# Half-contraction groups beside the first attention, and q of the second batch transposed on TensorE

## The chip, the cores and the metric

The kernel runs on one NeuronCore of one Trainium2 chip. The core has five engines that run side by side, each with its own instruction queue: TensorE (PE) for matrix products, VectorE (DVE), ScalarE (ACT), GpSimd (POOL) and SyncE (SP). Loads and stores (DMA) are issued by SP, ACT or POOL and are carried out by the core's 16 DMA engines. The metric is the device time of one execution in microseconds (us). Five timed runs of the kernel before gave a median of 305.79 us, from 305.18 to 306.97.

## What is computed

Eight batches of eight heads of linear attention are followed by a two-layer feed-forward network over all 4608 tokens. Cut to what matters:

```python
q_s = softmax(q, axis=-1)            # over the 64 of a head
k_s = softmax(k, axis=2)             # over the 576 positions
kv  = einsum('bhsd,bhse->bhde', k_s, v)
x   = einsum('bhsd,bhde->bhse', q_s, kv)   # then to (4608, 512)
h   = x @ w_in                       # 512 -> 2048
g   = where(h > 0, h, exp(min(h, 0)) - 1)
out = g @ w_out                      # 2048 -> 512
```

Inputs and output are 32-bit floats. The softmaxes are computed without the subtraction of the maximum, and the sum over k is taken as an extra column of ones in v.

## The kernel before

**Units and blocks.** Attention is cut into 16 units: unit n is half of batch n // 2, four heads. The feed-forward part is cut into nine blocks of 512 tokens. A batch has 576 tokens in nine chunks of 64, so the first block needs the first eight chunks of batch 0, and the second block the last chunk of batch 0 and most of batch 1.

**Elementwise work of a unit.** `q_part` takes the exp of q in place (ACT, L351), sums each row (DVE, L358) and takes the reciprocal (L363); `q_mul` multiplies and writes 16-bit QS (DVE, L374). `k_part` takes the exp of k (ACT, L394) and casts v to 16 bits, on POOL (L400) or on DVE (L403). To stand as a right-hand side, q must have its features on the partitions. For units 0 and 1 `tp` does that on PE: nine 128x128 transposes against an identity matrix (L420) into PSUM, and two evictions to qsT (L428). For all later units `q_mul` issues a DMA transpose on SP (L378), and `cvt` converts the result to qsT on POOL (L387).

**kv and attention of a unit.** `kv` does 36 small matmuls (L447); DVE takes the reciprocal of the sums (L460) and writes the scaled products into MBLK (two at L465). `ao` multiplies MBLK with qsT (L488) and evicts the result into XT, by ACT alone (L507) or with one half on ACT (L499) and one on DVE (L503). XT holds x transposed, as four contraction chunks (kc) of 128 features: unit 2b gives kc 0 and 1, unit 2b + 1 gives kc 2 and 3.

**A block.** `hg` makes one of eight groups: for two tiles of 128 hidden features, four matmuls each over kc 0 to 3 (L533), each 128x512. ACT takes exp (L541); POOL takes the minimum with 1 (L546) and DVE the rest of the elu (L549), or, in the first three groups of the first block, DVE does both (L553, L556). Then `out_mm` makes four output tiles, each over 16 hidden tiles (L566), in pieces of four matmuls; `out_store` evicts by ACT (L580) and stores by SP (L586). The next batch's kv and attention are put between the pieces of `out_mm`, at the places that the dictionary `work` gives.

**PSUM.** There are four tensors PS0 to PS3 of two banks each. They go round by name: hg's groups take A, Bs, C, Dd in turn, out takes A and Bs, and kv and attention of the next batch take C and Dd.

**The head.** SP loads q of unit 0 in two halves (L614), then q of unit 1 and k of unit 0 (L302). POOL loads v of unit 0, k and v of unit 1, W1 in twelve pieces (L314), then q2, q3, k2, v2, k3, v3 and W2 in four pieces of 1 MB (L324). PE fills waits with dummy matmuls on the identity (`spin`, L518).

**The order of the work.** Nothing is written out by hand but PE's order: `add` collects operations with a duration, a key and what they depend on, and `order` simulates the five queues with these durations and a model of the DMA rate. Each engine of the other four takes what could start first, and among those within 60 ns the one with the lowest key. Operations called `low` stand back for others that fall due. The resulting order is fixed in each engine's queue; on the chip, an engine that waits holds up all that stands behind it.

Of the kernel before, what the change touches and what calls it, by code (L numbers as in the profile page):

```python
# [19 lines left out]
ISSUE = {"sp": 600, "act": 650, "gp": 760}  # L20
W1CUT = (0, 2, 4, 8)


class Op:
    __slots__ = ("eng", "dur", "emit", "deps", "key", "idx", "start", "end",
                 "dma", "sem", "val", "clock", "nbytes", "follow", "low", "ready", "tag", "port", "slack", "rel")

# [7 lines left out]
class Sched:  # L35
# [5 lines left out]
    PGUARD = 0.3  # L41
    MARGIN = 2500
    DMA_RATE = 388.0
# [4 lines left out]
    def __init__(self, nc):  # L48
        self.nc = nc
        self.E = {"sp": nc.sync, "act": nc.scalar, "dve": nc.vector,  # L50
                  "pe": nc.tensor, "gp": nc.gpsimd}
        self.ops = []
        self.slack = False
        self.rel = None
        self.w = {}
        self.r = {}

    def add(self, eng, dur, emit, key, R=(), W=(), X=(), dma=None, nbytes=0, after=(),
# [3 lines left out]
        op.follow, op.low, op.tag, op.port = follow, low, tag, port  # L62
        op.slack = self.slack and low
        op.rel = self.rel if low else None
# [19 lines left out]
    def hop(self, d, o):  # L84
        if d.dma:
            return 60 + (self.MARGIN if o.slack else 0)
        if d.eng == o.eng:
            return 0 if o.eng == "pe" else 50
        if d.eng == "pe":
            return 210  # L90
        if o.eng == "pe":
            return 120
        return 70
# [32 lines left out]
    def one_pass(self, land):  # L126
# [27 lines left out]
        while left:  # L154
# [33 lines left out]
            if o.dma:  # L188
                o.end = max(s + self.DMA_GO[e] + self.DMA_TAIL + o.nbytes / self.DMA_RATE,
                            land.get(o, 0))  # L190
            out.append(o)
# [59 lines left out]
class Gen:  # L251
# [68 lines left out]
    def load_w2(self, s, key, follow=None):  # L320
        w = self.w_out.rearrange("(jj p) c -> p jj c", p=128)
        sl = slice(s * 4, (s + 1) * 4)
        return self.S.add(
            "gp", ISSUE["gp"], lambda e: e.dma_start(self.W2[:, sl, :], w[:, sl, :]), key,  # L324
            W=[f"W2_{s}"], dma=f"w2{s}", nbytes=1 << 20, follow=follow, tag=f"W2 {s}")

# [40 lines left out]
    def q_mul(self, n, key, dmat):  # L367
# [8 lines left out]
        if dmat:  # L376
            t16 = self.raw_flat(n, "q").bitcast(F16)[:, 0:1152].rearrange("p (c t) -> p c t", c=CH)
            S.add(dmat, 1400, lambda e: e.dma_start_transpose(  # L378
                t16, self.QS[al][:, :, :].rearrange("p c x -> p (c x)")), key,
                R=[f"QS{al}"], W=qR, dma=f"tp{i}{dmat}", nbytes=128 * 2304, low=True, tag=f"dtp{n}")  # L380

# [52 lines left out]
    def kv(self, units, ps, key):  # L434
# [17 lines left out]
        for n in units:  # L452
            i = n % 2
            R += [f"kR{i}", f"VB{i}0", f"VB{i}1", f"VBone{i}"]
        S.add("pe", len(units) * 300 + 330, mm, key, R=R, X=self.banks(ps), tag=f"kv{units}")
        PV = P[:, :].rearrange("p (f x) -> p f x", f=2)
# [21 lines left out]
    def ao(self, n, x, ps, key, evac="act"):  # L478
# [7 lines left out]
        for f in range(2):  # L486
            def mm(e, f=f):
                return e.matmul(P[:, f * 512:f * 512 + n_], M[:, f, :],  # L488
                                T[:, c0:c1, f * 64:f * 64 + 64], start=True, stop=True)
            S.add("pe", 230, mm, key,  # L490
                  R=[f"qsT{n % 2}{y}" for y in range(2)] + [f"MBLK{i}", f"MBLK{i}0", f"MBLK{i}1"],
                  X=[f"b{2 * ps + f}"], tag=f"ao{n}.{x}")
        src = P[:, :].rearrange("p (f t) -> p f t", f=2)[:, :, 0:n_]
        names = lambda f: [f"X{2 * u + f}_{(b * CH + c) % SLOTS}" for c in range(c0, c1)]
        if evac == "split":
            for f, eng in ((0, "act"), (1, "dve")):
# [11 lines left out]
              W=names(0) + names(1), X=self.banks(ps), tag=f"evx{n}")  # L508

    def spin(self, count, bk, after=None):
# [3 lines left out]
        def mm(e):  # L516
            for _ in range(count):
                last = e.matmul(dst, self.ID[:, :], self.ID[:, :], start=True, stop=True)  # L518
            return last
        self.S.add("pe", count * 57, mm, -5, R=["ID"], X=[f"b{bk}"],  # L520
                   after=[after] if after else (), tag="spin")

    def hg(self, j, g, ps, key, pool):
        S = self.S
        P = self.PS[ps]
        rc = BLK * (j % 3)
        xs = [f"X{kc}_{(8 * j + x) % SLOTS}" for kc in range(4) for x in range(8)]

        def mm(e):
            for t in range(2):  # L530
                tt = 2 * g + t
                for kc in range(4):
                    last = e.matmul(P[:, t * 512:(t + 1) * 512],  # L533
                                    self.W1[:, kc, tt * 128:(tt + 1) * 128],
                                    self.XT[:, kc, rc:rc + BLK], start=(kc == 0), stop=(kc == 3))
            return last
        self.pe = S.add("pe", 8 * 227, mm, key, R=xs + [f"W1_{kc}_{g}" for kc in range(4)], X=self.banks(ps), tag=f"hg{j}.{g}")
        i = self.eslot % len(self.ESB)
# [21 lines left out]
    def out_mm(self, jb, ts, bk, jj0, jj1, key):  # L560
# [3 lines left out]
        def mm(e):  # L564
            for jj in range(jj0, jj1):
# [4 lines left out]
              R=[f"G_{g}" for g in range(jj0 // 2, (jj1 + 1) // 2)] +  # L570
                [f"W2_{s}" for s in range(jj0 // 4, (jj1 + 3) // 4)], X=[f"b{bk}"],
              tag=f"out{jb}.{ts}.{jj0}")
# [32 lines left out]
    def program(self):  # L605
# [4 lines left out]
        for h in range(2):  # L610
# [4 lines left out]
                       W=[f"qR0h{h}"], dma=f"q0h{h}", nbytes=128 * 2304, follow=sp, tag="ld q0")  # L615
        for n, t in ((1, "q"), (0, "k")):
            sp = self.load(n, t, "sp", -89, follow=sp)
        gp = self.ident
        for n, t in ((0, "v"), (1, "k"), (1, "v")):
            gp = self.load(n, t, "gp", -80, follow=gp)  # L620
# [9 lines left out]
        self.q_mul(1, -63, None)  # L630
        self.k_part(0, -62)
        self.k_part(1, -64, vconv="dve")
        self.tp(0, 3, -64)
        self.spin(36, 0)
        self.kv([0], 2, -66)
        self.spin(9, 0)
        self.tp(1, 1, -64)
        self.spin(18, 0)
        self.kv([1], 3, -68)
        self.ao(0, 0, 0, -67, evac='split')  # L640
        self.ao(0, 1, 2, -60)
        self.ao(1, 0, 1, -67, evac="split")
        self.spin(6, 0)

        for what in ("2q", "3q", 0, "2k", "2v", 1, 2, "3k", "3v", 3):
            if isinstance(what, int):
                gp = self.load_w2(what, -50, follow=gp)
            else:
                gp = self.load(int(what[0]), what[1], "gp", -50, follow=gp)
        self.ldq, self.w2 = None, [gp]  # L650

        def loads(n, ts, key):
# [3 lines left out]

        def elem_q(b, key):
            for n in (2 * b, 2 * b + 1):
                self.q_part(n, key)
                if b != 2:  # L660
                    self.q_mul(n, key, "sp")

        def elem_k(b, key):
            for n in (2 * b, 2 * b + 1):
                self.k_part(n, key)

# [4 lines left out]
        key = 0  # L671
        A, Bs, C, Dd = 3, 0, 2, 1
        for j in range(NBLK):
            order = [A, Bs, C, Dd]
            for g in range(8):
                self.hg(j, g, order[g % 4], key, j or g > 2)
                key += 1
                if (j, g) == (0, 0):
                    self.ao(1, 1, 2, -66)
                    elem_q(1, 8)  # L680
                    elem_k(1, 8)
                    convert(1, 8)
            if j == 1:
# [8 lines left out]
            if b < B:  # L692
                n0, n1 = 2 * b, 2 * b + 1
                S.slack = True
                if more:
# [5 lines left out]

                def kv(units, b=b, C=C, more=more):
                    self.kv(units, C, key)
                    for n in units:
# [3 lines left out]

                def last(n1=n1, b=b, C=C, more=more):
                    self.ao(n1, 1, C, key)  # L710
                    if more and b > 1:
                        convert(b + 1, k1)
                todo = [lambda n=n0, d=Dd: self.ao(n, 0, d, key), lambda n=n0, c=C: self.ao(n, 1, c, key),
                        lambda n=n1, d=Dd: self.ao(n, 0, d, key), last]
                if j == 0:
                    work = dict(zip((6, 10, 11, 12, 13, 14),
                                    [lambda: kv([2]), lambda: kv([3])] + todo))
                else:
                    work = dict(zip((4, 12, 13, 14, 15) if j == 1 else (3, 6, 8, 9, 11), [lambda u=[n0, n1]: kv(u)] + todo))
            if j == 0:  # L720
                plan = [(ts, jq) for jq in range(4) for ts in range(4)]
            else:
                plan = [(ts + t, jq) for ts in (0, 2) for jq in range(4) for t in range(2)]
            bank = [2 * A, 2 * A + 1, 2 * Bs, 2 * Bs + 1]
            for k, (ts, jq) in enumerate(plan):
                self.out_mm(j, ts, bank[ts], 4 * jq, 4 * jq + 4, key)
                if jq == 3:
                    self.out_store(j, ts, bank[ts], key, last=(j, ts) == (NBLK - 1, 3))
                if k in work:
                    work[k]()  # L730
                key += 0.5
            if j == 0:
# [35 lines left out]
```

## Time and profile before

| what | us |
|---|---|
| median of five timed runs | 305.79 |
| the profiled execution's own time | 307.48 |
| its span, first to last instruction | 305.4 |
| start of the first block's groups (first L533) | 23.67 |
| start of the first out (first L566) | 38.75 |
| start of the second block's groups | 55.72 |
| PE busy over the span | 292.1 |

Times of rows count from the start of the span. In a timeline a row gives the start, the length, the engine, the line, the operation with the tiles that it writes and reads, and a count where several are merged; in brackets stands how long its engine stood idle before it and what ended that. Neighbouring matmuls overlap in such a row, since each is given with its latency. The chain of waits follows back, from the last instruction, what released each piece of work. PEclk is the clock granted to TensorE as a share of full speed.

### The profile page before, as it was taken

Reading aid. Unit: us, or ns where it says so; the run is one execution under the profiler, and the core shown is the slowest. Engines: PE = TensorE matmul, PEld = TensorE weight load, DVE = VectorE, ACT = ScalarE, POOL = GpSimd, SP = SyncE. Lnnn points to the kernel's source line nnn. Section 1 sums busy time; section 2 is a strip of 40 time slices with the busy share of each in tenths; the row PEclk is TensorE's granted clock in tenths of the full one; section 3 lists DMA queues with packets and bytes.
Section 4 is the critical chain, followed back from the end, with each engine's and each line's share of the span. In section 5 each row is a group of like instructions: output and inputs, shape, how many; then the busy total and the mean of one; then the engine's idle time right before and its main releaser. Section 6 shows DMA issues by size and latency. Waiting matters only on the chain.

```text
span 305.4 us, 4546 instructions
## 1 busy us (share of the span) xinstructions
PE 292.1 (96%) x1925; PEld 241.2 (79%) x1925; DVE 149.9 (49%) x181; ACT 151.2 (50%) x179; POOL 125.1 (41%) x128
## 2 busy tenths in 40 slices
PE   6389999999999999999999999999999999999994
PEld 6377878788888888888887888888888888888883
DVE  4345971189816770678057805790463046105600
ACT  3254922784475564565556455635552355125411
POOL 7691552183338422841284228504650045005500
PEclk9869999999999999999999999999999999999998
DMA  7999999950996099108950794069201220130032
GB/s 219 398 400 391 390 249 280 319 223 0 231 321 206 2 345 299 36 0 263 288 129 2 276 300 105 0 201 273 54 0 32 47 61 3 38 80 20 2 69 69
DMA packets 38116, 50.56 MB, mean 166 GB/s; under 512 B 18768, under 2 KB 18768, under 8 KB 38096
## 3 DMA queue, kind: packets, MB, share of 16 engines
q1 hardware_dynamic: 32880, 36.45, 42.8%
q0 software_dynamic: 5136, 13.70, 13.8%
q8 instruction: 15, 0.25, 0.3%
q10 hardware_dynamic: 80, 0.13, 0.2%
q14 instruction: 5, 0.04, 0.0%
HBM read 36.70 MB, written 9.44 MB: 151 GB/s over the span
## 4 chain that ended last, share of the span: by engine, by line
PE 93%; DMA 4%; ACT 1%; DVE 0%; SPq 0%; issue 0%
PE PS L566 44%; PE PS L533 43%; DMA KR<-in_k_dram 4%; PE PS L488 3%; PE PS L447 2%; PE PS L518 1%; ACT KR L394 0%; PE PS L420 0%; SPq L614 0%; DVE XT L503 0%; DVE MBLK L465 0%; ACT OSB L580 0%; SPq L302 0%; DVE RZK L460 0%
## 5 line engine op out<-in xcount | busy, mean ns | idle before, releaser
L549 DVE SCALAR_TENSOR_TENSOR GT<-ESB,PS 128x1024 fp32r<-128x1024 f32 x69 | 83.9, 1220 | 116.0 <-POOL ESB L546 115.9
L566 PE MATMUL PS<-W,GT 128*128 128x512 f32 x576 | 139.7, 392 | 0.0
L533 PE MATMUL PS<-XT,W 128*128 128x512 f32 x576 | 132.7, 390 | 0.4 <-DVE XT L503 0.4
L533 PEld LDWEIGHTS PS<-XT,W 128*128 128x128 f32 x576 | 107.8, 188 | 23.4 <-DVE XT L503 0.6
L566 PEld LDWEIGHTS PS<-W,GT 128*128 128x128 f32 x576 | 106.2, 188 | 20.9
L546 POOL TENSOR_SCALAR ESB<-ESB 128x1024 f32<-128x1024 f32 x69 | 72.0, 1044 | 95.8 <-ACT ESB L541 95.7
L541 ACT ACTIVATE ESB<-PS 128x1024 f32<-128x1024 f32 x72 | 74.0, 1028 | 54.1 <-PE PS L533 51.5
L580 ACT ACTIVATE OSB<-PS 128x512 f32<-128x512 f32 x36 | 21.5, 598 | 62.8 <-PE PS L566 62.5
L400 POOL CAST VB<-VR 128x1152 bf16<-128x1152 f32 x15 | 19.9, 1324 | 52.2 <-DMA VR<-in_v_dram 52.2
L358 DVE TENSOR_REDUCE ZQ<-QR 128x18 f32<-128x1152 f32 (+1 forms) x17 | 21.7, 1274 | 8.4 <-ACT QR L351 8.3
L507 ACT ACTIVATE XT<-PS 128x640 fp32r<-128x640 f32 (+4 forms) x30 | 18.7, 623 | 14.1 <-PE PS L488 14.0
L394 ACT ACTIVATE KR<-KR 128x1152 bf16<-128x1152 f32 x16 | 18.5, 1160 | 7.8 <-DMA KR<-in_k_dram 7.8
L374 DVE TENSOR_TENSOR QS<-QR,RZQ 128x1152 f16<-128x1152 f32 x16 | 22.1, 1393 | 0.4
L351 ACT ACTIVATE QR<-QR 128x1152 f32<-128x1152 f32 (+1 forms) x17 | 18.3, 1102 | 7.8 <-DMA QR<-in_q_dram 7.8
L387 POOL CAST qsT<-QR 128x1152 fp32r<-128x1152 f16 x14 | 16.5, 1179 | 13.9 <-DMA QR<-QS 13.8
L488 PEld LDWEIGHTS PS<-qsT,MBLK 128*128 128x128 f32 x64 | 11.9, 189 | 2.9 <-DVE MBLK L465 0.2
L488 PE MATMUL PS<-qsT,MBLK 128*128 128x320 f32 (+5 forms) x64 | 14.0, 303 | 0.1
L447 PEld LDWEIGHTS PS<-VB,KR 64*64 64x64 bf16 x576 | 5.7, 110 | 9.0 <-ACT KR L394 6.0
L518 PE MATMUL PS<-ID 128*128 128x128 f16 x115 | 10.8, 272 | 1.8 <-POOL ID L595 1.5
L447 PE MATMUL PS<-VB,KR 64*64 64x65 bf16 x576 | 6.8, 196 | 5.9 <-ACT KR L394 5.9
L518 PEld LDWEIGHTS PS<-ID 128*128 128x128 f16 x115 | 9.8, 126 | 2.4 <-POOL ID L595 1.5
L465 DVE TENSOR_TENSOR MBLK<-PS,RZK 64x128 fp32r<-64x128 f32 x32 | 9.3, 289 | 1.1
(26 smaller groups left out, 44.9 us busy)
## 6 DMA issues: line engine op xcount, KB each, us to landing
out_dram<-OSB SPq DMA_DIRECT2D x71, 128.0 KB, 2.6
QR<-in_q_dram SPq DMA_DIRECT2D x13, 576.0 KB, 8.0
KR<-in_k_dram SPq DMA_DIRECT2D x13, 576.0 KB, 5.5
VR<-in_v_dram SPq DMA_DIRECT2D x12, 576.0 KB, 6.4
W<-in_moe_w_out_dram POOLq DMA_DIRECT2D x4, 1024.0 KB, 20.3
VR<-in_v_dram POOLq DMA_DIRECT2D x4, 576.0 KB, 14.2
W<-in_moe_w_in_dram POOLq DMA_DIRECT2D x8, 256.0 KB, 12.2
W<-in_moe_w_in_dram POOLq DMA_DIRECT2D x4, 512.0 KB, 11.4
```

The lines of the kernel that those rows point to most:

```text
L358: S.add("dve", 750 if n == 0 else 1350, lambda e, zq=zq, src=src: e.tensor_reduce(zq, src, AX.X, ALU.add), key, R=res, W=[f"ZQ{i}" + (f"h{ ...
L374: S.add("dve", 1400, lambda e: e.tensor_tensor(qso, raw[:, :, :, :], rz, ALU.mult), key, R=qR + [f"RZQ{i}"], W=[f"QS{al}"], low=True, tag= ...
L400: self.cv[n] = S.add("gp", 1250, lambda e: e.tensor_copy(VB[:, :, :, 0:D], raw[:, :, :, :]), key, R=rv, W=[f"VB{i}0", f"VB{i}1"], low=True ...
L488: return e.matmul(P[:, f * 512:f * 512 + n_], M[:, f, :], T[:, c0:c1, f * 64:f * 64 + 64], start=True, stop=True)
L507: S.add("act", t_act(2 * n_, True), lambda e: e.activation(dst, src, AF.Copy), key, W=names(0) + names(1), X=self.banks(ps), tag=f"evx{n}")
L518: last = e.matmul(dst, self.ID[:, :], self.ID[:, :], start=True, stop=True)
L533: last = e.matmul(P[:, t * 512:(t + 1) * 512], self.W1[:, kc, tt * 128:(tt + 1) * 128], self.XT[:, kc, rc:rc + BLK], start=(kc == 0), stop ...
L541: S.add("act", t_act(1024, True), lambda e: e.activation(esb[:, :], P[:, :], AF.Exp), key, W=[f"E{i}"], X=self.banks(ps), tag=f"exp{j}.{g}")
L546: S.add("gp", 1120, lambda e: e.tensor_scalar(esb[:, :], esb[:, :], 1.0, 0.0, ALU.min, ALU.max), key, X=[f"E{i}"], tag=f"min{j}.{g}", port ...
L549: S.add("dve", t_dve(1024), lambda e: e.scalar_tensor_tensor(gt, esb[:, :], -1.0, P[:, :], ALU.add, ALU.max), key, R=[f"E{i}"], W=gw, X=se ...
L566: last = e.matmul(dst, GT[:, jj, ts * 128:(ts + 1) * 128], self.W2[:, jj, :], start=(jj == 0), stop=(jj == 15))
L580: S.add("act", t_act(512, True), lambda e: e.activation(osb[:, :], src, AF.Copy), key, W=[f"O{i}0", f"O{i}1"], X=[f"b{bk}"], tag=f"evo{jb} ...
```

## The change

In the first block, the first two groups of `hg` are made in two halves. The matmuls over kc 0 and 1, which need unit 0 alone, run before and after unit 1's attention, in PS3 and PS2; those over kc 2 and 3 follow in the same PSUM tensors. `ao_last` makes the ninth chunk of both units of batch 0 at once, with one eviction. The dummy matmuls between unit 1's transposes and the first group are left out, and unit 1's transposes come ahead of unit 0's kv. k of unit 0 is loaded by POOL instead of SP, ahead of the others.

For batch 1, q is transposed on PE by `tp`, inside the first block's out, in place of the DMA transposes and the casts on POOL; v of units 0, 2 and 3 is cast on DVE in place of POOL. W1 is loaded in sixteen pieces and W2 in five; the first MB of W2 is loaded ahead of q2 and q3. The first block's out is made in 20 pieces instead of 16, and the places of the next batch's work in the first two blocks move. The planner gets a term `late` by which it takes loads to land later, other durations for some PE operations, a slack of 1500 or 3500 ns in place of 2500 for some loads, and a lower key for the evictions of `ao`.

The diff, cut to its core:

```diff
-W1CUT = (0, 2, 4, 8)
+W1CUT = (0, 2, 4, 6, 8)
+W2CUT = (0, 4, 8, 12, 14, 16)
...
-            return 60 + (self.MARGIN if o.slack else 0)
+            return 60 + o.slack
...
-                            land.get(o, 0))
+                            land.get(o, 0)) + o.late
...
+    def ao_last(self, b, ps, key):
+        P, S = self.PS[ps], self.S
+        x = b * CH + CH - 1
+        for n in (2 * b, 2 * b + 1):
+            i = n % 2
+            def mm(e, i=i):
+                for f in range(2):
+                    last = e.matmul(P[:, f * 512 + i * 64:f * 512 + i * 64 + 64], self.MBLK[i][:, f, :],
+                                    self.qsT[i][:, CH - 1, f * 64:f * 64 + 64], start=True, stop=True)
+                return last
+            S.add("pe", 60, mm, key,
...
+        S.add("act", t_act(256, True), lambda e: e.activation(dst, src, AF.Copy), key,
+              W=[f"X{kc}_{x % SLOTS}" for kc in range(4)], X=self.banks(ps), tag=f"evx{b}")
...
-    def hg(self, j, g, ps, key, pool):
-        S = self.S
+    def hg_mm(self, j, g, ps, kcs, key=0):
...
-                for kc in range(4):
+                for kc in kcs:
                     last = e.matmul(P[:, t * 512:(t + 1) * 512],
                                     self.W1[:, kc, tt * 128:(tt + 1) * 128],
                                     self.XT[:, kc, rc:rc + BLK], start=(kc == 0), stop=(kc == 3))
...
+    def hg(self, j, g, ps, key, pool, kcs=(0, 1, 2, 3)):
+        S = self.S
+        P = self.PS[ps]
+        self.hg_mm(j, g, ps, kcs, key)
...
-        for n, t in ((1, "q"), (0, "k")):
-            sp = self.load(n, t, "sp", -89, follow=sp)
+            sp.late = 1300
+        self.load(1, "q", "sp", -89, follow=sp).late = 1000
         gp = self.ident
-        for n, t in ((0, "v"), (1, "k"), (1, "v")):
+        for n, t in ((0, "k"), (0, "v"), (1, "k"), (1, "v")):
             gp = self.load(n, t, "gp", -80, follow=gp)
...
-        self.k_part(0, -62)
-        self.k_part(1, -64, vconv="dve")
+        self.k_part(0, -69, vconv="dve")
+        self.k_part(1, -62, vconv="dve")
         self.tp(0, 3, -64)
-        self.spin(36, 0)
-        self.kv([0], 2, -66)
-        self.spin(9, 0)
-        self.tp(1, 1, -64)
-        self.spin(18, 0)
-        self.kv([1], 3, -68)
-        self.ao(0, 0, 0, -67, evac='split')
-        self.ao(0, 1, 2, -60)
-        self.ao(1, 0, 1, -67, evac="split")
-        self.spin(6, 0)
-
-        for what in ("2q", "3q", 0, "2k", "2v", 1, 2, "3k", "3v", 3):
+        self.spin(34, 6)
+        self.tp(1, 1, -71, evac="split")
+        self.kv([0], 2, -72)
+        self.spin(9, 6)
+        self.ao(0, 0, 0, -73, evac="split")
+        self.kv([1], 1, -74)
+        self.hg_mm(0, 0, 3, (0, 1))
+        self.ao(1, 0, 0, -75, evac="split")
+        self.hg_mm(0, 1, 2, (0, 1))
+        self.ao_last(0, 1, -60)
+        for what in (0, "2q", "3q", 1, "2k", "2v", 2, "3k", "3v", 3, 4):
...
+        for op in S.ops:
+            if op.dma and op.eng == "gp":
+                op.late = 2700
+        S.rel = self.pe
...
-                self.hg(j, g, order[g % 4], key, j or g > 2)
+                self.hg(j, g, order[g % 4], key, j or g > 2,
+                        (0, 1, 2, 3) if j or g > 1 else (2, 3))
                 key += 1
                 if (j, g) == (0, 0):
-                    self.ao(1, 1, 2, -66)
-                    elem_q(1, 8)
-                    elem_k(1, 8)
-                    convert(1, 8)
+                    elem_q(1, 8, None)
+                    elem_k(1, 8, "dve")
...
-                    work = dict(zip((6, 10, 11, 12, 13, 14),
-                                    [lambda: kv([2]), lambda: kv([3])] + todo))
+                    work = dict(zip((6, 8, 9, 11, 12, 13, 16, 17), (
+                        lambda: self.tp(2, C, key), lambda: self.tp(3, Dd, key),
+                        lambda: kv([2]), ao(2, 0, Dd), ao(2, 1, C),
+                        lambda: kv([3], Dd), lambda: self.ao(3, 0, C, key, evac="split"), last)))
                 else:
-                    work = dict(zip((4, 12, 13, 14, 15) if j == 1 else (3, 6, 8, 9, 11), [lambda u=[n0, n1]: kv(u)] + todo))
+                    work = dict(zip((5, 11, 12, 13, 14) if j == 1 else (3, 6, 8, 9, 11), (
+                        lambda: kv([n0, n1]), ao(n0, 0, Dd), ao(n0, 1, C), ao(n1, 0, Dd), last)))
             if j == 0:
-                plan = [(ts, jq) for jq in range(4) for ts in range(4)]
+                plan = [(ts, W2CUT[s], W2CUT[s + 1]) for s in range(5) for ts in range(4)]
```

## The prediction

> **What bounds the kernel.** I read the page first, then the chain of waits, then the timelines of the first 60 us, then the clock by windows.
>
> The page's busy row, and the head of its chain section:
>
> ```profile
> PE 292.1 (96%) x1925; PEld 241.2 (79%) x1925; DVE 149.9 (49%) x181; ACT 151.2 (50%) x179; POOL 125.1 (41%) x128
> ...
> PE 93%; DMA 4%; ACT 1%; DVE 0%; SPq 0%; issue 0%
> ```
>
> TensorE (PE) holds 93% of the chain. The rest lies at one place, the head. The chain in order of time (start, length, what):
>
> ```profile
> 2.14 13.06 DMA KR<-in_k_dram
> 15.22 1.17 ACT KR L394
> 16.44 0.71 PE PS L447 x19
> 17.15 1.07 PE PS L518 x9
> 18.22 0.96 PE PS L420 x9
> 19.18 1.63 PE PS L518 x18
> 20.81 0.45 PE PS L447 x34
> ...
> 22.16 0.74 PE PS L488 x2
> 22.93 0.70 DVE XT L503
> 23.67 2.12 PE PS L533 x8
> 25.79 0.14 PE PS L488 x2
> 25.94 12.81 PE PS L533 x56
> ```
>
> The last load of the head is k of unit 0, on SP's queue until 15.20. Behind it stand its exp, kv of unit 0, 9 dummy matmuls, unit 1's transposes, 18 more, kv and attention (L488) of unit 1, its eviction. Only then, at 23.67, does the first hidden group start, with all four contraction chunks (kc). From there PE never waits: asked for PE's waits after 25 us, the trace lists none. So the time is 23.67 us of head plus PE work. A change pays here only by starting the L533 stream earlier, by doing part of it inside the head, or by giving PE less; what it adds to PE is paid in full.
>
> PE is cold while it matters (window, PE busy, PEld, DVE, ACT, POOL, then PEclk, DMA share, GB/s):
>
> ```profile
> 14.00:16.00 2.00, 0.00 (x0) 0.00 (x0) 1.97 (x3) 0.78 (x1) 2.00 (x5) 0.50 1.29 384
> 16.00:18.00 2.00, 1.56 (x45) 1.49 (x46) 1.05 (x4) 1.44 (x2) 2.00 (x4) 0.50 1.26 399
> 18.00:20.00 2.00, 2.00 (x22) 2.00 (x20) 0.02 (x1) 0.78 (x2) 2.00 (x4) 0.50 1.21 408
> 20.00:22.00 2.00, 2.00 (x51) 1.68 (x48) 0.65 (x3) 0.71 (x2) 1.34 (x3) 0.91 1.17 409
> ```
>
> The clock is 0.50 until about 20.4, near four microseconds after PE resumed.
>
> **The loads of the head.** By their issues and landings: q0 lands at 3.5 and 4.6, q1 at 11.4, k0 at 15.2 (SP); v0 at 10.0, k1 at 12.4, v1 at 14.3, the first four W1 pieces at 15.4 to 18.9 (POOL). k0 moves to POOL's first place, and v0, k1 and v1 each move back one. Equal sizes, so by place: k0 10.0, v0 12.4; k1 and v1 replace the next 1.2 MB while SP no longer takes its 0.59 MB after 11.4, so I estimate 13.5 and 14.7. W1 stays where it is, as the sum ahead of it is the same. SP issues three loads instead of four; q1 still shares the engines with POOL, so 11.4. POOL loses the 1.15 us cast at 10.09, before which its queue stood 2.94 us; it gains four W1 issues and one W2 issue, at the 0.5 to 0.7 us between starts of its issues some 3 us. They end some 2 us after today's 23.8 at most, before the first minimum on POOL (32.81 today, about 29 then).
>
> **The new head, step by step.** q1 11.41, exp 1.16, reduction 1.35, reciprocal 0.27, multiply 1.36: the trace has QS at 15.66, unchanged. PE: transposes 15.75 to 16.7 (cold, 0.96), kv0 to 17.45 (0.71), nine dummies to 18.45. kv0 also needs v0's cast on DVE, 0.76 behind the multiply: 16.42, in time. DVE then has half of unit 1's transposed q, priced by the 128x512 PSUM cast (0.69), from 16.95, reciprocal 0.17, MBLK 0.61: 18.4, then v1's cast, 19.2. Attention of unit 0: 18.5 to 19.3 (2 x 0.43 cold), kv1 to 20.0; the evictions of unit 0 (ACT 0.60, DVE 0.69) end at 20.1. Half group (0,0), four matmuls of 0.229 (12.81 / 56): 20.2 to 21.1 with the clock back at 20.4. MBLK of unit 1 is ready at 21.0; attention of unit 1 to 21.55; half group (0,1) to 22.5 covers its eviction (22.4). The joint last chunk, four 64-column matmuls, two of which took 0.14 at 25.79: 0.3. **The second halves start at 22.8** with 8 of the 64 matmuls done.
>
> Gain: 23.67 - 22.8 = 0.9; 8 x 0.229 = 1.8; unit 1's last chunk, no longer at 25.79, 0.14. Together **2.85 us**.
>
> **What is added to PE.** q of units 2 and 3: 18 transposes. The nearest row (start, length, engine, line):
>
> ```profile
> 7.88 0.68 PE L420 MATMUL PS<-ID,QS 128*128 128x128 f16 x9 [0.92 <-DVE QS L374]
> 8.39 2.17 PE L518 MATMUL PS<-ID 128*128 128x128 f16 x36
> ```
>
> Warm, nine take 0.51 until the next matmul starts, so two sets cost 1.02. The Trainium skill, "TensorE: Matmul & The Clock Gate", section "Part 4: PE-mode transpose", speaks against the change: about 275 ns for one in a kernel's context, and transposes don't count as busy for the clock. By it, 18 x 275 = 4.95 us, and the sum would turn to a loss of 2.1. The row has 57 ns a piece; the 219 to 314 ns that the trace lists for a single one is its latency, not its spacing. I take 57, and keep 275 as the far end. Their four evictions (1.17 to 1.19 a pair) go to ACT, which today runs one exp between 39.8 and 51.3; the two SP transposes (2.98) and the two POOL casts (2.24) disappear off the path. DVE gains two v casts (1.52) between the elus; PE needs them at about 46.2 and 50, and v2 and v3 land by about 38.2 and 43.9.
>
> Finer cuts of out (20 pieces for 16) hold the same 64 matmuls: nothing. The later work places (j=1: kv a place later, attention one earlier, 0.93 us) cost nothing while the second converted q is ready: today it ends at 84.06 and is used at 85.67, so 0.7 us of cover is left; without it, up to 0.5.
>
> **Sum.** 2.85 - 1.02 = 1.8 us less. The profiled execution took 307.48 us with a span of 305.4: 303.6 and 305.7. The median of the timed runs, 305.79, is 1.7 below the profiled time, so **304.0 us**, 0.6% less. Under about 0.5% a measurement of this kernel can't tell a change from none.
>
> **Where the first block could stall.** One MB of W2 is now ahead of q2 and q3. W1 ends at 26.8; 1.05 MB at the 390 GB/s of these windows is 2.7 us, so W2's first piece lands about 29.5 (today 32.5), and q2 and q3 2.7 later than today's 28.3 and 29.7, 31.0 and 32.4; k3 and v3 keep 42.4 and 43.9. Meanwhile PE is about 2 us earlier. Today ACT takes q2's exp in order behind the third exp of the block:
>
> ```profile
> 29.72 1.03 ACT L541 ACTIVATE ESB<-PS 128x1024 f32<-128x1024 f32 x1 [0.78 <-PE PS L533]
> 30.64 1.16 ACT L351 ACTIVATE QR<-QR 128x1152 f32<-128x1152 f32 x1
> 31.70 1.01 ACT L541 ACTIVATE ESB<-PS 128x1024 f32<-128x1024 f32 x1
> ```
>
> The order comes from the planner, whose assumed landings the diff moves later (`late`), so I expect q2's exp to stand further back. PE's own order is fixed: out's five W2 pieces are wanted at about 35.9, 39.6, 43.8, 48.8 and 51.3 (0.93 for four L566 matmuls, with the inserted work) against landings that I estimate, by bytes again, at 29.5, 35.2, 40.9, 45.2 and 46.5.
>
> **The rivals.**
>
> *A, as summed* (48%): 304.0, own range 303.0 to 305.0.
>
> *B, the head stays cold* (19%). The same page, section "Part 1: The HAM clock gate", asks for a busy window of about 3.4 us whose phase runs free, and the new head has gaps where the old had 18 dummies. The trace agrees as far as it goes: 0.50 until 20.4 after a start at 16.44, transposes included. If the clock stays at 0.50 through both halves, half (0,0) ends at 21.85, attention of unit 1 at 22.7, half (0,1) at 24.4, and the second halves start 2.1 later: 306.1. Old heads suffer from a late window too; I put this case at 305.2.
>
> *C, the order stalls* (18%). Place: q2's exp kept between the third and fourth exp. After the shift that slot is at 27.6; the load comes at 31.0. The fourth exp then starts at 32.2 and ends 33.2, its minimum 34.25, its elu 35.5, and the last group, wanted at 34.0, waits 1.5; the fifth elu, behind q3's exp, adds 0.4 at the first out. 304.0 + 1.9 = 305.9, no change; each microsecond by which q2 is later adds one, up to 309. For it: the load is later, PE earlier. Against: q2 isn't wanted on PE before 42.4.
>
> *D, slower: the transposes cost the page's price* (4%). Place: after the seventh and ninth out piece, where PE has no cover. 305.79 - 2.85 + 4.95 = 307.9. From 158 ns each (2.85 / 18) the change loses. Against it stands the row's 57.
>
> *E, the head is shorter* (11%). If q1 comes earlier with k0 off its queue, q1 no longer ends last; v1 at 14.7, cast 0.76 and kv1 allow the second halves from about 21.4: 302.6. That k0's move does nothing, because q1's chain takes over, is already in A: it gives 0.9 only.
>
> **How the numbers follow.** Faster by over 0.5% is below 304.26: 0.31 of A, all of E, 0.03 of B: 0.45. Slower, above 307.3: D, a third of C, and 0.05 for what I haven't seen: 0.15. Same: 0.40. Range: E's value, widened by 0.2, up to most of C: 302.4 to 307.2; about one case in ten is left out above, less below.
>
> **What would show it.** After the change: the first L533-type matmuls near 20.2, a full unbroken stream from 22.8; kv0 after the transposes; two sets of nine transposes inside the first out, 0.5 each; the second block starting near 53.9 (55.72 - 1.8). A PE wait on an elu before the first out is C; PEclk 0.50 after 21 is B. I'm wrong at the root if q1 lands well off 11.4 or if PE waits anywhere after 23.

## The result, and the profile after

The changed kernel takes 303.67 us (median of 24 runs, 300.62 to 305.61) against 306.33 us for the kernel before (median of 43 runs, 304.48 to 307.80). Ratios here are taken over fast runs, which leaves out an execution over 1.5% above the fastest of its kernel: three of these 24, and of the experiments one in each of four kernels. The ratio is 0.9904, 95% interval 0.9884 to 0.9924: 0.96% or about 2.9 us less (2.7 by the two medians), where 0.6% and 1.8 us were forecast.

The profiled execution of the changed kernel has a span of 301.1 us and an own time of 302.94. That is 4.5 us below the 307.48 of the profiled execution before. The pair shows more than the medians do: the one before lies 1.15 us above its kernel's median, the one after 0.7 below its own.

The busy row of the page after, and the head of its chain section:

```profile
PE 291.1 (97%) x1917; PEld 240.2 (80%) x1917; DVE 153.7 (51%) x187; ACT 152.9 (51%) x181; POOL 122.5 (41%) x129
...
PE 94%; DMA 2%; DVE 1%; ACT 1%; SPq 0%; issue 0%
```

PE lost one microsecond of work and gained one point of share; the DMA share of the chain went from 4% to 2%, some 6 us. In the changed kernel L558 is a matmul of a group, L491 attention, L523 the joint last chunk, L450 kv, L598 out, L423 a transpose and L544 a dummy. The first block's chain in order of time (start, length, what):

```profile
1.67 6.61 DMA QR<-in_q_dram
...
8.30 1.16 ACT QR L354
9.47 0.60 ACT qsT L431
...
10.11 3.81 PE PS L544 x34
13.92 0.97 PE PS L423 x9
...
14.92 0.69 DVE qsT L434
...
17.27 0.70 DVE XT L507
...
18.01 1.20 PE PS L558 x4
19.21 0.46 PE PS L491 x2
19.68 0.92 PE PS L558 x4
20.60 0.37 PE PS L523 x4
20.96 12.79 PE PS L558 x56
33.75 6.35 PE PS L598 x28
40.10 0.52 PE PS L423 x9
...
42.50 0.52 PE PS L423 x9
```

The last load of the head is now q1, which landed at 8.28, not 11.4. Behind it stand its exp, and then something that the prediction did not have: an eviction of unit 0's transposed q (L431), and 34 dummies (L544) that waited for it. Both half groups (L558 x4), attention and the joint last chunk are near the sum. Nine dummies are still there between unit 1's transposes and the first half group, behind kv of unit 0. The second halves start at 20.96, and PE waits nowhere after it. Two sets of transposes (L423) take 0.52 each.

The 3.88 us by which the second block starts earlier (51.84 for 55.72) divide so: the stream starts 2.71 earlier, the groups after that point take 2.29 less (the first eight matmuls had taken 2.12 before, with their start), out with the transposes 1.12 more. The last 0.4 of the span lie in the second and third block, whose lengths were 31.43 and 31.36 before and are 31.22 and 31.16 after; the difference is in their groups, whose 64 matmuls took 14.80 and 14.71 before and 14.56 and 14.51 after. I didn't foresee that, and no run tests its cause.

### The profile page after: what moved, and what is told of

Read it like the earlier page. It is cut to its first block, busy times and chain, and to the rows that moved or that the text cites. A ratio compares the mean times of both kernels' runs of the same rounds, so it can differ in the third digit from the quotient of the medians.

```text
span 301.1 us, 4540 instructions
## 1 busy us (share of the span) xinstructions
PE 291.1 (97%) x1917; PEld 240.2 (80%) x1917; DVE 153.7 (51%) x187; ACT 152.9 (51%) x181; POOL 122.5 (41%) x129
## 4 chain that ended last, share of the span: by engine, by line
PE 94%; DMA 2%; DVE 1%; ACT 1%; SPq 0%; issue 0%
PE PS L598 44%; PE PS L558 44%; PE PS L491 3%; DMA QR<-in_q_dram 2%; PE PS L450 2%; PE PS L544 1%; PE PS L423 1%; ACT QR L354 0%; DVE VB L406 0%; SPq L646 0%; DVE XT L507 0%; DVE qsT L434 0%; ACT qsT L431 0%; ACT OSB L612 0%; DVE MBLK L468 0%
## 5 line engine op out<-in xcount | busy, mean ns | idle before, releaser
L598 PE MATMUL PS<-W,GT 128*128 128x512 f32 x576 | 140.4, 393 | 0.0
L558 PE MATMUL PS<-XT,W 128*128 128x512 f32 x576 | 132.6, 390 | 0.2 <-DVE XT L507 0.2
L558 PEld LDWEIGHTS PS<-XT,W 128*128 128x128 f32 x576 | 108.0, 188 | 22.8 <-DVE XT L507 0.3
L598 PEld LDWEIGHTS PS<-W,GT 128*128 128x128 f32 x576 | 106.0, 188 | 20.6
L403 POOL CAST VB<-VR 128x1152 bf16<-128x1152 f32 x12 | 15.6, 1301 | 45.1 <-DMA VR<-in_v_dram 45.1
L511 ACT ACTIVATE XT<-PS 128x640 fp32r<-128x640 f32 (+3 forms) x26 | 16.9, 652 | 14.8 <-PE PS L491 14.8
L390 POOL CAST qsT<-QR 128x1152 fp32r<-128x1152 f16 x12 | 13.8, 1152 | 7.0 <-DMA QR<-QS 7.0
L491 PE MATMUL PS<-qsT,MBLK 128*128 128x320 f32 (+4 forms) x60 | 13.5, 306 | 0.5 <-DVE MBLK L468 0.5
L491 PEld LDWEIGHTS PS<-qsT,MBLK 128*128 128x128 f32 x60 | 11.2, 189 | 3.2 <-DVE MBLK L468 0.7
L544 PE MATMUL PS<-ID 128*128 128x128 f16 x89 | 8.8, 285 | 3.4 <-ACT qsT L431 1.7
L544 PEld LDWEIGHTS PS<-ID 128*128 128x128 f16 x89 | 8.1, 133 | 3.9 <-ACT qsT L431 1.9
L315 POOL DMA_DIRECT2D W<-in_moe_w_in_dram x16 | 10.4, 1463 | 0.0
L326 POOL DMA_DIRECT2D W<-in_moe_w_out_dram x5 | 9.9, 2390 | 0.0
## 6 DMA issues: line engine op xcount, KB each, us to landing
W<-in_moe_w_out_dram POOLq DMA_DIRECT2D x3, 1024.0 KB, 18.6
VR<-in_v_dram POOLq DMA_DIRECT2D x4, 576.0 KB, 14.6
```

What stands on the lines that cost most here:

```text
L491: return e.matmul(P[:, f * 512:f * 512 + n_], M[:, f, :], T[:, c0:c1, f * 64:f * 64 + 64], start=True, stop=True)
L558: last = e.matmul(P[:, t * 512:(t + 1) * 512], self.W1[:, kc, tt * 128:(tt + 1) * 128], self.XT[:, kc, rc:rc + BLK], start=(kc == 0), stop ...
L598: last = e.matmul(dst, GT[:, jj, ts * 128:(ts + 1) * 128], self.W2[:, jj, :], start=(jj == 0), stop=(jj == 15))
```

## The experiments

Each kernel was timed beside the kernel before on the same chip. "Start" is the start of the second halves, or of the first whole group.

**k0 back on SP.**

```diff
-        self.load(1, "q", "sp", -89, follow=sp).late = 1000
+        sp = self.load(1, "q", "sp", -89, follow=sp)
+        sp.late = 1000
+        self.load(0, "k", "sp", -89, follow=sp).late = 2700
...
-        for n, t in ((0, "k"), (0, "v"), (1, "k"), (1, "v")):
+        for n, t in ((0, "v"), (1, "k"), (1, "v")):
```

> The changed kernel with k of unit 0 loaded by SP behind q1 again, and v0, k1, v1 first on POOL. All else as changed (the planner puts v0's cast ahead of q1's reciprocal, at most 0.8 us). Theory 1, the load order shortens the head: q1, alone on its queue, landed at 8.3 instead of 11.4 and k0 at 8.9 instead of 15.2; here q1 goes back to about 11 and k0 to about 15, the second half groups start at 23 to 23.5 instead of 20.96, ratio 0.997 to 1.000. Rival, the early q1 was one draw of a load whose landing varies from run to run anyhow: q1's landing and the ratio of 0.990 stay.

Ratio 0.990 (0.9856 to 0.9943), the changed kernel's own. q1 landed at 9.0, k0 at 13.5, start at 21.09. The theory that the load order had brought q1 forward falls. k0 was late, but kv0 now stands behind unit 1's transposes, which the dummies held until 14.6 anyway; k0's exp ended at 14.8, and the transposes at 15.1.

**Whole groups.**

```diff
-        self.hg_mm(0, 0, 3, (0, 1))
         self.ao(1, 0, 0, -75, evac="split")
-        self.hg_mm(0, 1, 2, (0, 1))
...
-                        (0, 1, 2, 3) if j or g > 1 else (2, 3))
+                        (0, 1, 2, 3))
...
-        S.rel = self.pe
+        S.rel = [o for o in S.ops if o.eng == "pe"][-1]
```

> The changed kernel without the half groups: the first two groups whole, after both units' attention. As predicted, the halves are worth 8 x 0.229 = 1.8 us: ratio 0.996. Rival, from the changed trace: the halves mostly fill waits that PE has in any case (for the eviction and for MBLK of unit 1), and without them unit 1's attention starts 0.5 earlier and the first group waits for its eviction until about 19.9: 64 matmuls from 19.9 instead of 56 from 20.96, a loss of 0.8 us only, ratio 0.993.

Ratio 0.9967 (0.9933 to 1.0000): 0.63% or about 1.9 us is lost, with an uncertainty of some 1.2 either way. The predicted 1.8 lies in it, and the 0.8 of the rival at its edge. The timeline shows where the first half group had stood (start, length, row, idle before), and the chain how long the groups took:

```profile
19.85 0.48 PE L450 MATMUL PS<-VB,KR 64*64 64x65 bf16 x36
21.29 1.12 PE L491 MATMUL PS<-qsT,MBLK 128*128 128x512 f32 x2 [0.96 <-DVE MBLK L468]
...
23.20 17.16 PE PS L558 x64
```

Unit 1's attention can't start before its MBLK, whether PE works meanwhile or not. But this profile has to be read with care. It is of the longest of the twelve executions, 309.5 us, which is not among those of the ratio (303.42 to 307.55). In it the granted clock fell back to 0.50 from 21.4 to 28.2, so that the 64 matmuls took 17.16 us instead of the 14.6 that they take at the changed kernel's rate (12.79 for 56). By an estimate from the mean clocks the other eleven had no such stretch: 6.8 us at half clock take 0.011 off the mean, which was 0.972 here and 0.983 to 0.989 in the others.

From q1's landing at 10.88 the second block (58.44) started after 47.6 us, or 45.0 without the 2.5 of the cold clock. With the halves it took 43.6 and 42.7 in the two profiles of the changed kernel. The 1.5 to 2.3 between them are nearer to the forecast than to the rival's 0.8: most of the halves fits into time that is waited in any case. One profile and this interval don't rule the rival out.

**q2 and q3 by DMA again.**

```diff
-                    elem_q(1, 8, None)
+                    elem_q(1, 8)
                     elem_k(1, 8, "dve")
+                    convert(1, 8)
...
-                    work = dict(zip((6, 8, 9, 11, 12, 13, 16, 17), (
-                        lambda: self.tp(2, C, key), lambda: self.tp(3, Dd, key),
+                    work = dict(zip((9, 11, 12, 13, 16, 17), (
```

> The changed kernel with q2 and q3 transposed by DMA on SP and converted on POOL again, no transposes on PE. As summed in the prediction, PE gets 1.0 us back: ratio 0.987, no new wait. Rival: with PE 3.9 us ahead of the kernel before, the DMA way is late (multiplies end 38.8 and 41.7, transposes 1.4 to issue and 5 to land, casts 1.2: 45 and 48 or later), attention of units 2 and 3, due at 45.5 and 49, waits for qsT: ratio 0.990 or above.

Ratio 0.9953 (0.9925 to 0.9980), 0.5% above the changed kernel, although PE does one microsecond less. Its chain shows what came in place:

```profile
39.23 1.36 DVE QS L377
40.59 0.03 DVE ZQ L361
40.62 6.16 DMA QR<-QS
46.78 0.06 issue
46.84 1.15 POOL qsT L390
47.99 0.04 issue
48.03 0.56 PE PS L491 x2
```

From the product to the converted q the DMA way takes 7.4 us, and PE waited 0.9 for it with a start at 22.79. In this one profile that about cancels the 1.04 saved (30.9 us from start to the second block, as in the changed kernel). An earlier start meets a longer wait, which is my reading of why the median loses; a profile with an early start was not taken of this kernel.

**k0 to POOL, alone, in the kernel before.**

```diff
-        for n, t in ((1, "q"), (0, "k")):
+        for n, t in ((1, "q"),):
...
-        for n, t in ((0, "v"), (1, "k"), (1, "v")):
+        for n, t in ((0, "k"), (0, "v"), (1, "k"), (1, "v")):
```

> The kernel before with one thing changed: k of unit 0 is loaded by POOL, ahead of v0, k1, v1, instead of by SP behind q1. Theory, k0's wait is real in the old order (kv of unit 0 stands ahead of unit 1's transposes and waited for k0 at 15.2): kv0 then starts at about 12.6, unit 1's transposes at q1's landing plus 4.3, the first group at about 21.5 instead of 23.67, ratio 0.993. Rival, as in the changed kernel, where moving k0 back cost nothing: what ends last is q1's chain in any case, ratio 0.998 to 1.000.

Ratio 1.0019 (0.9987 to 1.0051): nothing, as the rival says, but not for the rival's reason. In the profile q1 landed at 6.3 and k0 was out of the way, so the first group started at 17.68, six microseconds early. The second block started at 55.47, only 0.25 early. The chain in the first out:

```profile
33.28 5.32 PE PS L566 x24
38.61 9.02 DMA QR<-QS
47.62 0.05 issue
47.67 1.16 POOL qsT L387
48.84 0.04 issue
48.88 0.90 PE PS L488 x2
49.78 1.71 PE PS L566 x4
```

The first DMA transpose was issued at 38.6 instead of 43.5, but landed after 9.0 us instead of 5.4: at 47.6 instead of 48.9. The loads of batch 1 and W2 were still running: the engines moved 376 to 402 GB/s until 42, and 79 from 43 to 44. PE waited, by the trace's list of its waits:

```profile
PE PS L488 <- POOL qsT L387: 3.4, 1, 3.4
```

and was cold after it (granted clock 0.50 from 49 to 52; four out matmuls in 1.71 for 0.93).

**Transposes on PE in the kernel before, alone and with k0's move.**

```diff
-                    elem_q(1, 8)
+                    for n in (2, 3):
+                        self.q_part(n, 8)
+                        self.q_mul(n, 8, None)
                     elem_k(1, 8)
-                    convert(1, 8)
...
-                    work = dict(zip((6, 10, 11, 12, 13, 14),
-                                    [lambda: kv([2]), lambda: kv([3])] + todo))
+                    work = dict(zip((5, 6, 8, 10, 11, 12, 13, 14),
+                                    [lambda d=Dd: self.tp(2, d, key), lambda: kv([2]),
+                                     lambda d=Dd: self.tp(3, d, key), lambda: kv([3])] + todo))
```

The second kernel also has the load edit of the one above.

> The kernel before with q2 and q3 transposed on PE inside the first out (unit 2 after the sixth, unit 3 after the ninth piece) instead of by DMA and POOL's casts; the old head, loads and dummies. As summed in the prediction, PE pays 1.0 us for the 18 transposes and nothing comes back: ratio 1.003. Rival: in the kernel before, the DMA transposes land only when the loads thin out (at 47 to 49, whenever they are issued), so each execution whose head is earlier than 23.67 gives that back at attention of unit 2; with the transposes on PE it keeps it: ratio 0.993 to 0.998, and times spread wider downward than those of the kernel before.

> The same, and k of unit 0 first on POOL. Theory: moving k0 alone gave nothing (1.002) because the 6 us that the head gained (first group at 17.68) came back as a wait of 3.4 us for qsT and slower pieces; with the transposes on PE the earlier head is kept: ratio 0.988 or below. Rival, another late load (W2's last piece, v3) takes the wait's place: ratio 0.995 or above, with a wait of PE in the first out.

Alone: 1.0040 (1.0004 to 1.0075), a loss of 1.2 us, in agreement with the 1.0 of the sum; the rival falls. In the old head k0, behind q1, keeps the start late (k0 at 13.7, start 21.65 in this profile), so there was little to give back. Together: 0.9944 (0.9919 to 0.9969), 1.7 us less, though less than the 0.988 expected. The chain, in which PE no longer waits after 20:

```profile
19.83 2.13 PE PS L533 x8
...
34.92 5.44 PE PS L566 x24
40.35 0.52 PE PS L420 x9
...
44.33 0.52 PE PS L420 x9
...
53.07 7.09 PE PS L533 x30
```

Neither edit gains anything by itself; the pair does. In this profile q1 landed at 9.87, and the second block started 43.2 us after it, between the 43.6 and 42.7 of the changed kernel. So to that point two edits of the diff do as well as all of it, in one profile. The ratios differ by 0.4% or 1.2 us, of which the profiles show 0.6 us, in the second and third block (31.43 and 31.59 for 31.22 and 31.16).

**The dummies of the head.**

```diff
# spin_bank0
-        self.spin(34, 6)
+        self.spin(34, 0)
# spin_22
-        self.spin(34, 6)
+        self.spin(22, 6)
# spin_exp
-        self.spin(34, 6)
+        self.spin(34, 0)
+        self.spin(24, 0, after=self.exp_q)
```

> The changed kernel with the 34 dummy matmuls after unit 0's transposes writing bank 0, free since the start, instead of bank 6, which unit 0's transposed q still occupies until ACT has evicted it behind q1's exp. Theory: in the changed trace the dummies started at 10.11, 1.7 us after the transposes, ran cold for 3.8 us and held unit 1's transposes until 13.92, though QS was ready at 12.55. Here they run from about 8.4 warm to 10.4, and unit 1's transposes start at 12.6: 1.3 us off the head, ratio 0.986. Rival: the cold dummies pay for themselves by waking the clock (1.00 from about 15.2); without them it is 0.50 until about 18 or later, and the head gains nothing: ratio 0.990 or above.

> The changed kernel with 22 instead of 34 dummies in the place after unit 0's transposes, on bank 6 as changed. They start 1.8 us after q1's landing and take 0.107 each cold, so 34 end 5.6 us after it and 22 end 4.3 us after it, when QS of unit 1 is ready. Theory, the dummies hold unit 1's transposes up: 1.3 us less than the changed kernel, ratio 0.986, and PE starts the transposes cold but is warm by the half groups. Rival, the 12 dummies paid for themselves by the clock: ratio 0.990.

> The changed kernel with 22 dummies on bank 6, once more, for a narrower interval: 0.986 to 0.988 if the dummies held the head up by 1.3 us, 0.990 or above if the first look was a lucky draw of q1's landing.

> The changed kernel with 34 dummies on free bank 0 right after unit 0's transposes and 24 more that start when the exp of q1 ends: 24 x 0.107 = 2.6 us cold, done 3.8 us after q1's landing, QS is ready 4.3 after it. Theory: it keeps what 22 dummies on bank 6 and bank 0 alone each gave and wakes the clock 0.6 us earlier than the former: ratio 0.986. Rival: no better than 22 on bank 6, 0.988.

| kernel | ratio | interval | q1 lands | start | start - q1 |
|---|---|---|---|---|---|
| changed | 0.9904 | 0.9884 to 0.9924 | 8.28 | 20.96 | 12.7 |
| changed, again | 0.9917 | 0.9880 to 0.9954 | 10.64 | 22.44 | 11.8 |
| spin_bank0 | 0.9868 | 0.9824 to 0.9912 | 10.70 | 22.60 | 11.9 |
| spin_22 | 0.9880 | 0.9831 to 0.9928 | 6.1 | 19.35 | (13.3) |
| spin_22, again | 0.9872 | 0.9835 to 0.9910 | 9.31 | 21.08 | 11.8 |
| spin_exp | 0.9864 | 0.9814 to 0.9913 | 10.13 | 21.31 | 11.2 |

(In the first profile of spin_22 q1 came so early that unit 0's chain ended last.) All four ratios lie below both of the changed kernel, by 0.2 to 0.5%, but the intervals overlap: likely a gain of about one microsecond, not a proved one. Nor do the starts prove it: behind q1, only that of spin_exp is clearly earlier than the 11.8 of the changed kernel's second profile. In spin_exp PE waits for QS again, and not QS for PE:

```profile
8.36 4.75 PE L544 MATMUL PS<-ID 128*128 128x128 f16 x58
14.45 0.68 PE L423 MATMUL PS<-ID,QS 128*128 128x128 f16 x9 [1.35 <-DVE QS L377]
```

Without late dummies (spin_bank0) the transposes start right at QS too, but the granted clock is 0.50 from about 15.2 to 18.6, which takes part of it back.

**The changed kernel again.**

> The changed kernel itself, on the same chip as the others, as their reference and as another look at where q1 lands. Ratio 0.990. If q1's landing sets the head, q1 lands somewhere from 8 to 11.5 and the second half groups start 12.6 to 12.7 us after it.

Start came 11.8 after q1, not 12.6; the clock woke earlier within the dummies (34 in 3.47 us, not 3.81). Between the two profiles q1 and the start moved the same way, by 2.4 and 1.5.

**q1 with the engines to itself.**

```diff
-        sp = None
+        sp = first = None
...
             sp.late = 1300
+            first = first or sp
...
-            gp = self.load(n, t, "gp", -80, follow=gp)
+            gp = self.load(n, t, "gp", -80, follow=gp, after=[first])
```

> The changed kernel with POOL's first load waiting for the landing of q0's first half (about 3.5 us) instead of starting at 1.7, so that q1 has the DMA engines to itself until about 6. Theory, q1's landing (8.3 to 10.9 in the changed kernels) sets the head and is late because it shares with POOL's loads: q1 lands at 6 to 7, the second half groups start about 3 us earlier if no other load takes over, ratio 0.983 or less. Rival, what q1 gains k0, v0 and v1 lose by starting 2 us later, and v1's chain (v1 at 14 or later, cast, kv1, MBLK, attention) ends last: ratio 0.988 to 0.993.

Ratio 0.990 (0.9854 to 0.9945): the rival. q1 landed at 7.2, and v1, issued by POOL at 6.36, at 15.86. Its cast, then kv1 on a PE that had idled back to half clock, then the first half group at half speed (2.07 for 1.20; the granted clock was 0.50 until 21):

```profile
15.88 0.90 DVE VB L406
...
16.83 0.71 PE PS L450 x29
...
17.55 2.07 PE PS L558 x4
19.62 0.85 PE PS L491 x2
20.48 1.21 PE PS L558 x4
21.68 0.37 PE PS L523 x4
22.05 3.98 PE PS L558 x17
```

So six loads are needed before the start, and what one gains another loses. That q1 is late because it shares isn't shown: 7.2 lies within the 6.1 to 10.9 of the profiles in which it shares.

## Why the prediction was right, and where its working was not

**The size and the sign.** 304.0 was forecast, 303.67 measured, in a range of 302.4 to 307.2; the case A held. That the two times are so near is partly luck. The forecast started from 305.79, the median of five, where 43 runs give 306.33; from there the same sum leads to 304.5, and the gain was half as large again as the sum. (In the sum, 303.6 belongs to the span and 305.7 to the profiled time.)

**The half groups, 1.8 us.** Borne out: 1.9 when they are undone, give or take 1.2.

**The transposes' price, 1.02 us.** Right: 0.52 a set, and 1.2 us when they alone are added to the kernel before (0.1 to 2.3 by the interval). Rival D, by the 275 ns a piece of the Trainium skill ("TensorE: Matmul & The Clock Gate", "Part 4: PE-mode transpose"), is out: issued in a stream they cost 57 ns.

**"the two SP transposes (2.98) and the two POOL casts (2.24) disappear off the path".** This step failed. They are off the path only in the profile of before, whose head was late. With a start at 17.68 they ended last, and PE waited 3.4. I costed the transposes as a pure addition; with an early head they are what lets its gain through.

**The head.** 22.8 lies 1.8 and 0.4 above the two starts of the changed kernel (20.96 and 22.44). That it is so near is luck: two errors partly cancel. First, *"PE: transposes 15.75"*: I had the dummies run right after unit 0's transposes, as before. They now write bank 6, which unit 0's transposed q occupies until ACT has evicted it, and ACT does that behind q1's exp. So they start 1.8 after q1 and hold PE for 3.8 cold; with q1 at 11.41 the start would have been at 23.2 to 24.1. Second, *"q1 still shares the engines with POOL, so 11.4"*: the trace of before was an extreme draw. In the other twelve profiles with POOL's loads starting at 1.7, q1 lands between 6.1 and 10.9, most often from 9 to 10.7, whichever queue carries k0. I had read one landing as a constant. By the prediction's own sign, q1 well off 11.4, its head was wrong at the root. Nor is it shown that the new head is shorter at all: the old one started at 21.65 in the profile with the transposes alone, between the two starts of the new.

**The 0.9 that k0's move was to give.** Alone in the kernel before it gives nothing; together with the transposes on PE 1.7; in the changed kernel undoing it costs nothing, since the dummies hide k0 (its exp ended at 14.8, the transposes behind them at 15.1). Such a share belongs to the set of edits, not to one.

**B, C and E.** The clock was back at 1.00 by 15.0 in the changed kernel (columns as in the prediction, PEclk third from last), so B did not come:

```profile
14.00:16.00 2.00, 1.90 (x54) 1.49 (x51) 1.05 (x3) 1.08 (x2) 2.00 (x6) 0.79 1.34 390
16.00:18.00 2.00, 1.22 (x38) 0.67 (x38) 1.90 (x5) 1.27 (x2) 2.00 (x5) 1.00 1.26 384
```

C did not either: the planner put q2's exp behind the sixth exp, not the third, with the load at 30.0 (31.0 forecast):

```profile
30.16 1.03 ACT L573 ACTIVATE ESB<-PS 128x1024 f32<-128x1024 f32 x1 [0.78 <-PE PS L558]
31.08 1.16 ACT L354 ACTIVATE QR<-QR 128x1152 f32<-128x1152 f32 x1
```

E's early q1 is there in the first profile of the changed kernel (8.28) and hardly in the second (10.64); its cause, k0 off the queue, is not borne out, since q1 came at 9.0 with k0 behind it.

**Why the gain is larger than 1.8.** By the prediction's prices, halves and transposes give 0.8 us (1.8 less 1.0). Undone in the changed kernel, each for itself, they cost 1.9 and 1.5 us, with uncertainties of 1.2 and 1.0: together as much as the whole gain of 2.9. The transposes were priced at a loss and are worth a gain, since with the DMA transposes an early start runs into a wait. How much of the rest is the head, where the old one waits for the later of q1 and k0 and the new one for q1, the runs don't separate; 0.4 in blocks two and three stays unexplained. Nor does a run undo by itself the order of unit 1's transposes and unit 0's kv, the casts of v on DVE, the order and cuts of the W loads, or the planner's new terms.

## What to carry to other kernels

A head that gets earlier is worth only what the next fixed arrival lets through: find the transfer that does not move with it, here a DMA transpose that lands when the loads thin out, and change the two together. A filler is not free because it fills a wait: ask which buffer it writes and what must be evicted from there first. And a landing read from one profile is one draw; before it goes into a sum as a constant, a second execution is needed.

## What was not expected of the hardware

The landing of the same 576 KB load, issued at 1.66 beside POOL's stream, lay anywhere from 6.1 to 11.4 us over thirteen executions; with POOL's first load held back by 2.3 us it was 7.2. A DMA transpose issued 4.9 us earlier took 9.0 instead of 5.4 us and landed 1.3 earlier. A PE that idled for 3.35 us took 1.71 us for four out matmuls that take 0.93 warm. And in the longest execution with whole groups the clock fell to 0.50 at 21.4, though PE's last wait had been 0.96 us only, and stayed there for 6.8 us.
